# A planned attention stage: keeping VectorE's and GpSimd's SBUF work apart, one scan for the states, new ranks

## The chip, the cores and the metric

One core of one Trainium2 chip. The metric is the device time of one execution in microseconds (us). The kernel before takes 622.71 us, the median of three runs (622.52 to 623.51).

## The reference, cut to what matters

A decaying linear attention is followed by two feed-forward layers, all in 32-bit floats. Batch 2, 8 heads, 768 steps, head size 64; after it 1536 tokens of width 512.

```python
for t in range(S):                       # attention, decay gamma per head
    state = gamma * state + outer(k[t], v[t])
    y[t] = scale * (q[t] @ state)
x = y as (1536, 512)
h = x @ w_in                             # 512 -> 2048
x = where(h > 0, h, exp(min(h, 0)) - 1) @ w_out        # 2048 -> 512
out = ((x @ w_a) * (x @ w_b)) @ w_o      # 512 -> 1536 -> 512
```

## The kernel before

The recurrence is cut into 6 chunks of 128 steps. Heads go in 8 pairs (4 pairs per batch), two heads on the 128 partitions. For a pair, `decay` (ScalarE, L405) scales the keys, `states` (TensorE, L412) makes the sum of each of the first five chunks in PSUM as a block of 64 columns, `first` (ScalarE, L422) copies the first block to SBUF, and `scan` (VectorE, L427) carries the decay over the other four with four instructions in a row. For each half of a pair (three chunks), `scores` (TensorE, L454) makes the products of queries and keys, `masked` (VectorE, L460) multiplies them by a decay mask, `result` (TensorE, L475 with the states and L481 with the values) sums the output in PSUM, and `decayed` (VectorE, L491) writes it to SBUF as `yf`. `part` then splits `yf` into a high part (ScalarE, L513) and a low part (GpSimd, L517, a subtraction that reads and writes SBUF); the two are the operand of the dense layers.

The dense layers multiply in three products per block (L579 to L581: high by high, high by low, low by high), each of 128 by 128 by 512. Their weights come as 64-bit words, and every tile of 128 by 512 has to be rebuilt in 32 bits: two ScalarE passes (L348, L349), then four VectorE passes whose operands all lie in SBUF, `clamp` (L353), `shift` (L357), `join` (L361), `total` (L368), then a ScalarE pass (L374, high part) and a GpSimd subtraction (L378, low part). A tile is fetched by `fetch` (SyncE's DMA queue, L343) into one of three buffers, which `join` sets free.

The order of the attention stage is computed by a planner (`Plan`, L79) while the program is built. Every step is an operation with an engine, a cost, a rank (its due time), what it follows and the buffers that it takes. `run` picks again and again the operation that can start first by its model; an operation of the same engine with a lower rank that could start within 0.25 us of it goes before it. The model only sets the order of instructions within each engine and in SyncE's queue `Q`; on the chip the engines wait for data and buffers alone. The planner holds the 8 pairs, the first 8 weight tiles (`2 * G`; four of `w1`, four of `w2`), and `tile_f`: the first four blocks of the first dense layer (48 products), ranks 100 and above, which fill in where TensorE has nothing else. A pair `p` has the base rank 6 + 5.6 p, weight tile j the rank `need(j)` (L335), its steps some way before that. The cost model knows nothing of one engine slowing another.

After the planner, the dense loops run (`moe`, L705) with their own order by hand. They rebuild the other 60 weight tiles (`w_steps`, L183) between the products, with the tiles fetched by `w_load` (L172), up to three ahead.

Of the kernel before, what the change touches and what calls it, by code (L numbers as in the profile page):

```python
# [19 lines left out]
P = 128  # L20
C = 128
# [51 lines left out]
class Op:  # L73
    def __init__(self, engine, cost, rank, emit, after, takes, users):
        self.engine, self.cost, self.rank, self.emit = engine, cost, rank, emit
        self.after, self.takes, self.users, self.end = after, takes, users, None


class Plan:  # L79
# [4 lines left out]


    LAG = {"Q": 1.6}

    def __init__(self):
        self.ops = []

    def op(self, engine, cost, rank, emit, after=(), takes=(), uses=()):

        o = Op(engine, cost, rank, emit, [a for a in after if a], [t[0] for t in takes], [t[1] for t in takes])
        for users in [*o.users, *uses]:
            users.append(o)
        self.ops.append(o)
        return o
# [14 lines left out]
    def run(self, begin):  # L112
        clock, left = dict(begin), list(self.ops)
        while left:
            best = None
            for o in left:
                t = self.ready(o)
                if t is None:
                    continue
                t = max(t, clock[o.engine])  # L120
                key = (t, o.rank)
                if best is None or key < best[0]:
                    best = key, o
            (t, _), o = best

            for p in left:
                if p.engine == o.engine and p.rank < o.rank:
                    tp = self.ready(p)
                    if tp is not None and max(tp, clock[o.engine]) <= t + 0.25:
                        o = p  # L130
            t = max(t, self.ready(o))
            picked = []
            for rings, users in zip(o.takes, o.users):
                ring = min((r for r in rings if r.free_at() is not None), key=lambda r: r.free_at())
                ring.homes.append(users)
                picked.append(ring)
            o.end = t + o.cost
            clock[o.engine] = o.end
            left.remove(o)
            o.emit(*picked)  # L140
        return clock
# [3 lines left out]
def tile_kernel(ctx: ExitStack, tc: tile.TileContext, qk, kv, w1, w2, wa, wb, wo, tab, out):  # L145
# [23 lines left out]
    state = {"loaded": 0, "split": 0, "read": 0, "freed": 0, "tick": 0, "quota": 0, "lag": 0, "room": NW // 2}  # L169
    NS = 3  # L170

# [84 lines left out]
    def attention():  # L256
        pool, PS = tc.tile_pool, bass.MemoryType.PSUM
        with (
# [9 lines left out]
            mask = cst.tile([P, H, C], F32, name="mask")  # L268
            zero = cst.tile([P, 3 * C], F32, name="zero")
            nc.vector.memset(zero, 0.0)  # L270
            causal = tb1[:, :C]
            rise = lambda h: tb1[:, C + h : C + h + 1]
# [5 lines left out]
            warm = ps_s.tile([P, 2, 512], F32, tag="sc", name="warm")  # L278
            for _ in range(2):
                nc.tensor.matmul(warm[:, 0, : 3 * C], zero[:, :C], zero, start=True, stop=True)  # L280

            plan = Plan()
            op = plan.op
            ring = {n: Ring(k) for n, k in dict(qk=3, kv=3, kd=2, a=3, st=2, yf=2, raw=3, da=2, dc=2, du=2, m=3, r=3).items()}
            rsc, ry, r0 = Ring(2), Ring(2), Ring(2)
# [48 lines left out]

            need = lambda j: 32.0 + 3.5 * j if j < G else 60.0 + 3.0 * (j - G)  # L335

            def weight(j):
# [41 lines left out]

                o = op("Q", 1.3, n - 14, fetch, takes=[([ring["raw"]], raw_)])  # L380
                o = op("ACT", 1.3, n - 8, words, [o], [([ring["da"]], a_), ([ring["dc"]], c_)], [raw_])
                o = op("DVE", 0.5, n - 7, clamp, [o], uses=[a_])
                o = op("DVE", 0.6, n - 6.5, shift, [o], uses=[a_])
                o = op("DVE", 0.9, n - 6, join, [o], [([ring["du"]], u_)], [a_, raw_])
                o = op("DVE", 0.8, n - 5, total, [o], uses=[u_, c_])
                o = op("ACT", 0.6, n - 4, high, [o], uses=[u_])
                done["w", key] = op("POOL", 1.3, n - 3, low, [o], uses=[u_])


            def pair(p):  # L390
                b, hp = divmod(p, NHP)
                z = base(p)
                if b == 0:
                    done["mask", hp] = op(
                        "ACT", 0.7, z - 4,
                        lambda: [nc.scalar.mul(mask[:, h], causal, rise(h)) for h in (2 * hp, 2 * hp + 1)], [t1_],
                    )
                Q, K = users["qk", p], users["kv", p]
                kd_, s_, st_ = [], [], []

                def decay():
                    kd = tile_of(("kd", p), at, [P, NCH, 2, D], "kd")
                    k_ = T["kv", p][:, 0].rearrange("p (c h d) -> p c h d", c=NCH, h=2)
                    for h in range(2):
                        nc.scalar.mul(kd[:, :, h, :], k_[:, :, h, :], gk(2 * hp + h))  # L405

                def states(r):
                    ps = (ps_y if r is ry else ps0).tile([P, 512], F32, tag="y" if r is ry else "p", name="yk")
                    T["s", p] = ps = ps[:, : (NCH - 1) * D].rearrange("p (c d) -> p c d", d=D)
                    for c in range(NCH - 1):  # L410
                        for h in range(2):
                            nc.tensor.matmul(  # L412
                                ps[h * D : (h + 1) * D, c, :],
                                T["kd", p][:, c, h, :],
                                T["kv", p][:, 1, c * P + h * D : c * P + (h + 1) * D],
                                start=True,
                                stop=True,
                            )

                def first(*_):  # L420
                    st = tile_of(("st", p), at, [P, NCH - 1, D], "st")
                    nc.scalar.copy(st[:, 0, :], T["s", p][:, 0, :])  # L422

                def scan():
                    st, ps = T["st", p], T["s", p]
                    for c in range(1, NCH - 1):
                        nc.vector.scalar_tensor_tensor(  # L427
                            out=st[:, c, :], in0=st[:, c - 1, :], scalar=gc(hp), in1=ps[:, c, :],
                            op0=ALU.mult, op1=ALU.add,
                        )  # L430

                o = op("ACT", 1.15, z - 3, lambda *_: decay(), [done["k", p], t1_], [([ring["kd"]], kd_)], [K])
                o = op("PE", 0.75, z + 1, states, [o, done["v", p]], [([ry, r0], s_)], [kd_, K])
                o = op("ACT", 0.3, z + 1.1, first, [o], [([ring["st"]], st_)], [s_])
                done["st", p] = op("DVE", 1.25, z + 1.5, scan, [o], uses=[st_, s_])

                for half in range(2):
                    half_of(p, half, st_)

            def half_of(p, half, st_):  # L440
# [26 lines left out]
                def result(r):  # L467
# [3 lines left out]
                    for i in range(3):  # L471
                        c = half * 3 + i
                        for h in range(2 if c else 0):
                            r_ = slice(h * D, (h + 1) * D)
                            nc.tensor.matmul(  # L475
                                y[r_, i, :], st[r_, c - 1, :], q_[r_, c * C : (c + 1) * C], start=(c in (1, 3)), stop=False
                            )
# [21 lines left out]
                o = op("DVE", 0.95, z + 0.5, masked, [o, done["mask", hp]], [([ring["a"]], a_)], [sc_])  # L499
                o = op("PE", 1.5 + 0.2 * half, z + 6.5, result, [o, done["st", p]], [([ry, r0], y_)], [a_, st_, Q, K])  # L500
                done["y", key] = o
# [7 lines left out]
            def part(p, blk, key, o, yf_, cols, from_, rank):  # L509
# [10 lines left out]
                o = op("ACT", 0.2 + n / 1280, rank, high, [o, blk == NB - 1 and done["y", (NHP - 1, 1)]], uses=[yf_])  # L520
                done["x", blk, key] = op("POOL", 0.25 + n / 500, rank, low, [o], uses=[yf_])


            def tile_f(f, rank):
# [38 lines left out]
                o = op("ACT", 0.6, 43 + rank, high, [o], uses=[r_])  # L563
                op("POOL", 1.3, 45 + rank, low, [o], uses=[r_])

            with pool(name="atA", bufs=3) as atA:
                for p in range(NPAIR):
                    pair(p)
                for j in range(2 * G):
                    weight(j)  # L570
                for f in range(G):
                    tile_f(f, 4 * f)
                plan.run({"Q": 2.2, "PE": 4.2, "DVE": 1.4, "ACT": 2.3, "POOL": 0.4})
            state.update(loaded=2 * G, split=2 * G, read=2 * G)

# [188 lines left out]
```

## Time and profile before

| | |
|---|---|
| median of three runs | 622.71 us |
| profiled execution, its own time | 623.38 us |
| its span, first to last instruction | 621.6 us |
| TensorE busy in the span | 610.1 us, 98% |
| VectorE, ScalarE, GpSimd busy | 359.8, 285.4, 255.7 us |
| mean granted TensorE clock | 0.994 |

The profile is that of one execution; 1.8 us of its time lie outside of the span. A matmul's record ends with the end of its pipeline, so that records overlap: the distance between starts is what it costs in a row of others. The rows of a timeline begin with the start and the duration in us; in brackets stands how long the engine was idle before, and what ended that. A 32-bit matmul of the attention leaves two records.

### The profile page before, as it was taken

What the parts mean: (1) busy time and instruction counts of PE and PEld (TensorE: products, weight loads), DVE (VectorE), ACT (ScalarE), POOL (GpSimd) and SP (SyncE); (2) the same over time, 40 slices, a digit from 0 to 9 for tenths busy, and PEclk for the clock granted to TensorE, in tenths of its full rate; (3) what the DMA queues carried; (4) which work ended last, traced back from release to release, by engine and by line L of the source; (5) the groups of instructions that cost most, each with busy time, mean ns of one, the idle gap of its engine ahead of it and who ended that gap; (6) DMA issues with size and microseconds to landing.
All of it is one profiled execution on the core that took longest, in us unless ns stands there. A gap on an engine that the chain in (4) does not pass through costs nothing.

```text
span 621.6 us, 8081 instructions
## 1 busy us (share of the span) xinstructions
PE 610.1 (98%) x3168; PEld 503.5 (81%) x3168; DVE 359.8 (58%) x482; ACT 285.4 (46%) x514; POOL 255.7 (41%) x192
## 2 busy tenths in 40 slices
PE   7989899999999999999999999999999999999997
PEld 5867688888888888888888888888888888888886
DVE  2899856787784378528891282767065677211122
ACT  4574776778554457536752253444242444121110
POOL 0355654566455236516774352435133334311110
PEclk9999899999999999999999999999999999999999
DMA  8972413333321033202330031233022130001002
GB/s 325 408 280 67 130 39 97 103 102 102 102 74 62 1 102 101 69 1 69 101 101 2 1 100 37 71 98 101 1 67 69 49 93 30 0 2 51 18 34 102
DMA packets 14838, 52.24 MB, mean 84 GB/s; under 512 B 1616, under 2 KB 2512, under 8 KB 14800
## 3 DMA queue, kind: packets, MB, share of 16 engines
q1 hardware_dynamic: 14368, 50.99, 25.6%
q10 hardware_dynamic: 432, 0.73, 0.3%
q8 instruction: 25, 0.41, 0.3%
q14 instruction: 13, 0.11, 0.1%
HBM read 48.57 MB, written 3.15 MB: 83 GB/s over the span
## 4 chain that ended last, share of the span: by engine, by line
PE 91%; DVE 5%; DMA 1%; issue 1%; ACT 0%; SPq 0%; DVEq 0%
PE p L579 30%; PE p L581 30%; PE p L580 30%; DMA qk<-in_qk 1%; PE sc L454 1%; DVE a L460 1%; DVE yf L491 1%; DVE a L357 1%; DVE st L427 1%; DVE a L353 1%; PE yk L481 1%; DVE u L368 1%; PE yk L475 1%; DVE u L361 1%; SPq L315 0%
## 5 line engine op out<-in xcount | busy, mean ns | idle before, releaser
L603 POOL TENSOR_TENSOR gl<-pr,gh 128x512 fp32r<-128x512 f32 x36 | 50.5, 1403 | 156.9 <-ACT gh L601 156.9
L579 PE MATMUL p<-yh,wh 128*128 128x512 f32 x288 | 112.0, 389 | 0.0
L580 PE MATMUL p<-yl,wh 128*128 128x512 f32 x288 | 112.0, 389 | 0.0
L581 PE MATMUL p<-yh,wl 128*128 128x512 f32 x288 | 112.0, 389 | 0.0
L208 POOL TENSOR_TENSOR wl<-u,wh 128x512 fp32r<-128x512 f32 x60 | 88.3, 1472 | 51.7 <-ACT wh L206 50.8
L603 POOL TENSOR_TENSOR gl<-r,gh 128x512 fp32r<-128x512 f32 x44 | 67.2, 1528 | 81.4 <-ACT gh L601 81.4
L667 DVE TENSOR_TENSOR pr<-p,sa 128x512 f32<-128x512 f32 x36 | 24.9, 691 | 111.2 <-PE p L581 111.2
L201 DVE CUSTOM_DVE_ANT_0 u<-u,c 128x1024 uint16<-128x1024 uint16 x60 | 77.3, 1288 | 2.8
L579 PE MATMUL p<-xh,wh 128*128 128x512 f32 x192 | 75.6, 394 | 2.0 <-DVE r L546 2.0
L581 PE MATMUL p<-xh,wl 128*128 128x512 f32 x192 | 75.4, 393 | 0.0
L580 PE MATMUL p<-xl,wh 128*128 128x512 f32 x192 | 75.2, 392 | 0.0
L579 PE MATMUL p<-gh,wh 128*128 128x512 f32 x192 | 74.7, 389 | 0.0
L580 PE MATMUL p<-gl,wh 128*128 128x512 f32 x192 | 74.7, 389 | 0.0
L581 PE MATMUL p<-gh,wl 128*128 128x512 f32 x192 | 74.7, 389 | 0.0
L194 DVE TENSOR_SCALAR a<-a 128x512 f32<-128x512 f32 x60 | 65.3, 1088 | 15.9 <-ACT a L190 15.7
L601 ACT CAST gh<-pr 128x512 fp32r<-128x512 f32 x36 | 22.4, 621 | 101.5 <-DVE pr L667 101.5
L580 PEld LDWEIGHTS p<-yl,wh 128*128 128x128 f32 x288 | 54.1, 188 | 11.3
L579 PEld LDWEIGHTS p<-yh,wh 128*128 128x128 f32 x288 | 54.1, 188 | 11.2
L581 PEld LDWEIGHTS p<-yh,wl 128*128 128x128 f32 x288 | 54.1, 188 | 11.1
L580 PE MATMUL p<-wl,gh 128*128 128x512 f32 (+1 forms) x148 | 56.7, 383 | 0.0
L581 PE MATMUL p<-wh,gl 128*128 128x512 f32 (+1 forms) x148 | 56.7, 383 | 0.0
L579 PE MATMUL p<-wh,gh 128*128 128x512 f32 (+1 forms) x148 | 56.7, 383 | 0.0
(63 smaller groups left out, 946.6 us busy)
## 6 DMA issues: line engine op xcount, KB each, us to landing
raw<-in_w SPq DMA_DIRECT2D x32, 512.0 KB, 3.6
raw<-in_wa SPq DMA_DIRECT2D x12, 512.0 KB, 3.8
raw<-in_wb SPq DMA_DIRECT2D x12, 512.0 KB, 3.7
raw<-in_wo SPq DMA_DIRECT2D x12, 512.0 KB, 3.8
qk<-in_qk SPq DMA_DIRECT2D x7, 768.0 KB, 6.6
kv<-in_kv SPq DMA_DIRECT2D x7, 768.0 KB, 9.1
out<-oacc SPq DMA_DIRECT2D x11, 256.0 KB, 2.0
qk<-in_qk SPq DMA_DIRECT2D x2, 384.0 KB, 5.1
```

Of the source, the lines that this page charges most:

```text
L194: nc.vector.tensor_scalar(a, a, E_LO, E_HI, op0=ALU.max, op1=ALU.min)
L201: nc.vector.tensor_tensor(out=u, in0=u, in1=c, op=ALU.add)
L208: nc.gpsimd.tensor_tensor(out=lo, in0=t, in1=hi.bitcast(F32), op=ALU.subtract)
L353: nc.vector.tensor_scalar(a, a, E_LO, E_HI, op0=ALU.max, op1=ALU.min)
L357: nc.vector.tensor_single_scalar(ai, ai, 3, op=ALU.logical_shift_left)
L361: nc.vector.scalar_tensor_tensor(out=u, in0=T["raw", j][:, :, 1], scalar=SIGN, in1=T["da", j].bitcast(I32), op0=ALU.bitwise_and, op1=ALU.b ...
L579: nc.tensor.matmul(ps, lh, rh, start=first, stop=False)
L580: nc.tensor.matmul(ps, lh, rl, start=False, stop=False)
L581: nc.tensor.matmul(ps, ll, rh, start=False, stop=last)
L601: nc.scalar.copy(hi, t)
L603: nc.gpsimd.tensor_tensor(out=lo, in0=t, in1=hi.bitcast(F32), op=ALU.subtract)
L667: nc.vector.tensor_tensor(out=pr, in0=pb, in1=sa, op=ALU.mult)
```

## The change

- The planner knows a port: VectorE's four weight passes and all of GpSimd's subtractions are marked with it, and no two marked operations may overlap in its clock. On the chip no wait is added; what changes is the order in each engine.
- A TensorE operation of a rank below 100 may not be taken while it is more than 3 ranks above the lowest rank left on TensorE. An operation of a lower rank goes first if it could start within 0.1 us (before 0.25).
- The states of a pair come from one scan instruction of VectorE over 320 elements, which reads PSUM and a row of rates. For that `states` writes them with the chunk as the innermost index (a step of 20 bytes), the states lie so in SBUF too, and `result` reads them with that step as its stationary operand. ScalarE's copy of the first block goes; a ScalarE operation that writes the rates of a pair (`rate`, 320 elements) comes.
- `need` becomes 22 + 4.5 j for the first four weight tiles (before 32 + 3.5 j) and is lowered by 10 for the next four. 11 tiles are fetched in the planner (before 8); 8 are still rebuilt there.
- The costs in the model are lowered a little for the weight passes, and the six warm-up products of 128 columns stand for two of 384.

```diff
+    AHEAD, FILL = 3, 100
...
     def run(self, begin):
-        clock, left = dict(begin), list(self.ops)
+        clock, left = dict(begin, port=0.0), list(self.ops)
+        open_ = lambda o: max(clock[o.engine], clock["port"] + 0.05 if o.port else 0.0)
         while left:
             best = None
+            last = min((o.rank for o in left if o.engine == "PE"), default=0) + self.AHEAD
+            far = lambda o: o.engine == "PE" and last < o.rank < self.FILL
             for o in left:
                 t = self.ready(o)
-                if t is None:
+                if t is None or far(o):
                     continue
-                t = max(t, clock[o.engine])
+                t = max(t, open_(o))
...
-                if p.engine == o.engine and p.rank < o.rank:
+                if p.engine == o.engine and p.rank < o.rank and not far(p):
                     tp = self.ready(p)
-                    if tp is not None and max(tp, clock[o.engine]) <= t + 0.25:
+                    if tp is not None and max(tp, open_(p)) <= t + 0.1:
                         o = p
-            t = max(t, self.ready(o))
+            t = max(t, self.ready(o), open_(o))
...
             clock[o.engine] = o.end
+            if o.port:
+                clock["port"] = o.end
...
-    NS = 3
+    NS, NPL = 3, 8
...
-            zero = cst.tile([P, 3 * C], F32, name="zero")
+            zero = cst.tile([P, C], F32, name="zero")
             nc.vector.memset(zero, 0.0)
+
+            one = cst.tile([P, D * (NCH - 1)], F32, name="one")
+            nc.vector.memset(one, 1.0)
+            nc.vector.memset(one.rearrange("p (d c) -> p d c", c=NCH - 1)[:, :, 0], 0.0)
...
-            for _ in range(2):
-                nc.tensor.matmul(warm[:, 0, : 3 * C], zero[:, :C], zero, start=True, stop=True)
+            for i in range(6):
+                nc.tensor.matmul(warm[:, 0, i % 3 * C : (i % 3 + 1) * C], zero, zero, start=True, stop=True)
...
-            need = lambda j: 32.0 + 3.5 * j if j < G else 60.0 + 3.0 * (j - G)
+            need = lambda j: 22.0 + 4.5 * j if j < G else 50.0 + 3.0 * (j - G)
...
                 o = op("Q", 1.3, n - 14, fetch, takes=[([ring["raw"]], raw_)])
+                if j >= NPL:
+                    raw[key] = j
+                    return
                 o = op("ACT", 1.3, n - 8, words, [o], [([ring["da"]], a_), ([ring["dc"]], c_)], [raw_])
-                o = op("DVE", 0.5, n - 7, clamp, [o], uses=[a_])
-                o = op("DVE", 0.6, n - 6.5, shift, [o], uses=[a_])
-                o = op("DVE", 0.9, n - 6, join, [o], [([ring["du"]], u_)], [a_, raw_])
-                o = op("DVE", 0.8, n - 5, total, [o], uses=[u_, c_])
+                o = op("DVE", 0.44, n - 7, clamp, [o], uses=[a_], port=True)
+                o = op("DVE", 0.44, n - 6.5, shift, [o], uses=[a_], port=True)
+                o = op("DVE", 0.7, n - 6, join, [o], [([ring["du"]], u_)], [a_, raw_], True)
+                o = op("DVE", 0.65, n - 5, total, [o], uses=[u_, c_], port=True)
                 o = op("ACT", 0.6, n - 4, high, [o], uses=[u_])
-                done["w", key] = op("POOL", 1.3, n - 3, low, [o], uses=[u_])
+                done["w", key] = op("POOL", 1.3, n - 3, low, [o], uses=[u_], port=True)
...
-                    T["s", p] = ps = ps[:, : (NCH - 1) * D].rearrange("p (c d) -> p c d", d=D)
+                    T["s", p] = ps = ps[:, : (NCH - 1) * D]
+                    ps = ps.rearrange("p (d c) -> p d c", c=NCH - 1)
...
-                                ps[h * D : (h + 1) * D, c, :],
+                                ps[h * D : (h + 1) * D, :, c],
...
+                def rate(*_):
+                    nc.scalar.mul(tile_of(("keep", p), at, [P, D * (NCH - 1)], "keep"), one, gc(hp))
+
+                def scan(*_):
+
+                    st = tile_of(("st", p), at, [P, D, NCH - 1], "st")
+                    nc.vector.tensor_tensor_scan(
+                        st.rearrange("p d c -> p (d c)"), T["keep", p], T["s", p], 0.0, ALU.mult, ALU.add
+                    )
...
+                e = op("ACT", 0.55, z - 2.5, rate, [t1_], [([ring["keep"]], ke_)])
                 o = op("PE", 0.75, z + 1, states, [o, done["v", p]], [([ry, r0], s_)], [kd_, K])
-                o = op("ACT", 0.3, z + 1.1, first, [o], [([ring["st"]], st_)], [s_])
-                done["st", p] = op("DVE", 1.25, z + 1.5, scan, [o], uses=[st_, s_])
+                done["st", p] = op("DVE", 0.81, z + 1.5, scan, [o, e], [([ring["st"]], st_)], [s_, ke_])
...
-                                y[r_, i, :], st[r_, c - 1, :], q_[r_, c * C : (c + 1) * C], start=(c in (1, 3)), stop=False
+                                y[r_, i, :], st[r_, :, c - 1], q_[r_, c * C : (c + 1) * C], start=(c in (1, 3)), stop=False
...
-                for j in range(2 * G):
+                for j in range(NPL + NS):
                     weight(j)
...
-            state.update(loaded=2 * G, split=2 * G, read=2 * G)
+            raw.update({k: T["raw", j] for k, j in raw.items()})
+            state.update(loaded=NPL + NS, split=NPL, read=NPL)
```

## Rows read from the trace of the kernel before

**Rows 1.** Busy time by stretch: stretch, length, PE, PEld, DVE, ACT, POOL busy (instructions), clock, DMA share, GB/s.

```profile
16.00:24.00 8.00, 8.00 (x134) 6.71 (x132) 5.57 (x13) 4.10 (x11) 3.15 (x4) 1.00 1.01 409
24.00:66.86 42.86, 38.33 (x520) 30.95 (x517) 40.87 (x72) 25.52 (x57) 22.65 (x26) 0.96 0.57 207
...
38.60:47.60 9.00, 6.87 (x92) 5.71 (x94) 8.11 (x15) 6.10 (x14) 4.91 (x6) 0.81 0.52 183
...
100.00:200.00 100.00, 100.00 (x443) 82.81 (x442) 75.52 (x97) 67.00 (x116) 55.85 (x38) 1.00 0.31 90
```

**Rows 2.** TensorE's waits from 16 to 67 us: total us, times, longest.

```profile
PE p L579 <- DVE r L546: 2.0, 1, 2.0
PE sc L454 <- DVE a L460: 1.8, 2, 1.3
```

**Rows 3.** Timeline of TensorE around its idle time at 44 us.

```profile
36.04 0.80 PE L412 MATMUL yk<-kv,kd 128*64 128x64 f32 x20
36.77 0.65 PE L475 MATMUL yk<-qk,st 64*64 64x128 f32 x8
...
38.72 0.94 PE L454 MATMUL sc<-qk 64*128 64x128 f32 x12 [0.49 <-DVE a L460]
...
44.41 1.65 PE L454 MATMUL sc<-qk 64*128 64x128 f32 x12 [1.34 <-DVE a L460]
45.98 1.33 PE L412 MATMUL yk<-kv,kd 128*64 128x64 f32 x20
```

**Rows 4.** Timeline of TensorE after its idle time at 65 us, first dense products.

```profile
67.91 0.43 PE L580 MATMUL p<-xl,wh 128*128 128x512 f32 x1
...
71.55 0.40 PE L580 MATMUL p<-xl,wh 128*128 128x512 f32 x1
```

**Rows 5.** VectorE's groups from 0 to 76 us: busy us, mean ns of one, idle before.

```profile
L491 DVE TENSOR_TENSOR yf<-yk,gy 128x384 f32<-128x384 f32 x16 | 8.8, 550 | 2.4 <-PE yk L481 2.1
L361 DVE SCALAR_TENSOR_TENSOR u<-raw,a 128x512 int32<-128x512 int32 x8 | 8.1, 1006 | 0.8 <-issue 0.5
L368 DVE CUSTOM_DVE_ANT_0 u<-u,c 128x1024 uint16<-128x1024 uint16 x8 | 7.5, 939 | 0.2
L353 DVE TENSOR_SCALAR a<-a 128x512 f32<-128x512 f32 x8 | 6.2, 780 | 0.0
L357 DVE TENSOR_SCALAR a<-a 128x512 int32<-128x512 int32 x8 | 5.7, 716 | 0.1
```

**Rows 6.** Timeline of VectorE and GpSimd: passes beside each other, and passes alone.

```profile
27.52 0.41 DVE L357 TENSOR_SCALAR a<-a 128x512 int32<-128x512 int32 x1
27.96 0.69 DVE L361 SCALAR_TENSOR_TENSOR u<-raw,a 128x512 int32<-128x512 int32 x1
28.22 1.30 POOL L517 TENSOR_TENSOR xl<-yf,xh 128x384 fp32r<-128x384 f32 x1 [1.37 <-ACT xh L513]
28.57 1.22 DVE L427 SCALAR_TENSOR_TENSOR st<-st,tb,yk 128x64 f32<-128x64 f32 x4
...
38.53 1.28 POOL L378 TENSOR_TENSOR wl<-u,wh 128x512 fp32r<-128x512 f32 x1 [1.28 <-ACT wh L374]
38.59 1.50 DVE L353 TENSOR_SCALAR a<-a 128x512 f32<-128x512 f32 x1
...
42.79 0.69 DVE L368 CUSTOM_DVE_ANT_0 u<-u,c 128x1024 uint16<-128x1024 uint16 x1
```

**Rows 7.** ScalarE's groups from 0 to 67 us: busy us, mean ns of one, idle before.

```profile
L405 ACT ACTIVATE kd<-kv,tb 128x384 f32<-128x384 f32 x16 | 8.9, 607 | 4.0 <-DMA kv<-in_kv 4.0
L348 ACT ACTIVATE a<-raw 128x512 f32<-128x512 f32 x7 | 4.7, 674 | 0.0
L374 ACT CAST wh<-u 128x512 fp32r<-128x512 f32 x6 | 3.7, 620 | 4.7 <-DVE u L368 4.6
```

**Rows 8.** Timeline: pair 4's keys after their transfer, and its states.

```profile
26.39 1.12 ACT L405 ACTIVATE kd<-kv,tb 128x384 f32<-128x384 f32 x2 [0.47 <-DMA kv<-in_kv]
...
32.01 0.75 PE L412 MATMUL yk<-kv,kd 128*64 128x64 f32 x20
```

More of the change, by code (lines that the diff above doesn't have):

```diff
@@ L73, with __init__ @@
 class Op:
-    def __init__(self, engine, cost, rank, emit, after, takes, users):
+    def __init__(self, engine, cost, rank, emit, after, takes, users, port):
         self.engine, self.cost, self.rank, self.emit = engine, cost, rank, emit
-        self.after, self.takes, self.users, self.end = after, takes, users, None
+        self.after, self.takes, self.users, self.port, self.end = after, takes, users, port, None
 class Plan:
+    AHEAD, FILL = 3, 100
     LAG = {"Q": 1.6}
@@ L89, in __init__, with op @@
         self.ops = []
-    def op(self, engine, cost, rank, emit, after=(), takes=(), uses=()):
-        o = Op(engine, cost, rank, emit, [a for a in after if a], [t[0] for t in takes], [t[1] for t in takes])
+    def op(self, engine, cost, rank, emit, after=(), takes=(), uses=(), port=False):
+        o = Op(engine, cost, rank, emit, [a for a in after if a], [t[0] for t in takes], [t[1] for t in takes], port)
         for users in [*o.users, *uses]:
@@ L278, in attention @@
             warm = ps_s.tile([P, 2, 512], F32, tag="sc", name="warm")
-            for _ in range(2):
-                nc.tensor.matmul(warm[:, 0, : 3 * C], zero[:, :C], zero, start=True, stop=True)
+            for i in range(6):
+                nc.tensor.matmul(warm[:, 0, i % 3 * C : (i % 3 + 1) * C], zero, zero, start=True, stop=True)
             plan = Plan()
             op = plan.op
-            ring = {n: Ring(k) for n, k in dict(qk=3, kv=3, kd=2, a=3, st=2, yf=2, raw=3, da=2, dc=2, du=2, m=3, r=3).items()}
+            ring = {n: Ring(k) for n, k in dict(qk=3, kv=3, kd=2, keep=2, a=3, st=2, yf=2, raw=3, da=2, dc=2, du=2, m=3, r=3).items()}
             rsc, ry, r0 = Ring(2), Ring(2), Ring(2)
@@ L398, in pair @@
                 Q, K = users["qk", p], users["kv", p]
-                kd_, s_, st_ = [], [], []
+                kd_, s_, st_, ke_ = [], [], [], []
                 def decay():
@@ L418, in states @@
                             )
[L420 to L430, printed above, removed]
+                def rate(*_):
[5 more added lines that the diff above has]
+                    )
                 o = op("ACT", 1.15, z - 3, lambda *_: decay(), [done["k", p], t1_], [([ring["kd"]], kd_)], [K])
+                e = op("ACT", 0.55, z - 2.5, rate, [t1_], [([ring["keep"]], ke_)])
                 o = op("PE", 0.75, z + 1, states, [o, done["v", p]], [([ry, r0], s_)], [kd_, K])
-                o = op("ACT", 0.3, z + 1.1, first, [o], [([ring["st"]], st_)], [s_])
-                done["st", p] = op("DVE", 1.25, z + 1.5, scan, [o], uses=[st_, s_])
+                done["st", p] = op("DVE", 0.81, z + 1.5, scan, [o, e], [([ring["st"]], st_)], [s_, ke_])
                 for half in range(2):
@@ L499, in half_of @@
                 o = op("DVE", 0.95, z + 0.5, masked, [o, done["mask", hp]], [([ring["a"]], a_)], [sc_])
-                o = op("PE", 1.5 + 0.2 * half, z + 6.5, result, [o, done["st", p]], [([ry, r0], y_)], [a_, st_, Q, K])
+                o = op("PE", 1.45 + 0.25 * half, z + 6.5, result, [o, done["st", p]], [([ry, r0], y_)], [a_, st_, Q, K])
                 done["y", key] = o
@@ L520, in part @@
                 o = op("ACT", 0.2 + n / 1280, rank, high, [o, blk == NB - 1 and done["y", (NHP - 1, 1)]], uses=[yf_])
-                done["x", blk, key] = op("POOL", 0.25 + n / 500, rank, low, [o], uses=[yf_])
+                done["x", blk, key] = op("POOL", 0.25 + n / 500, rank, low, [o], uses=[yf_], port=True)
             def tile_f(f, rank):
@@ L563, in tile_f @@
                 o = op("ACT", 0.6, 43 + rank, high, [o], uses=[r_])
-                op("POOL", 1.3, 45 + rank, low, [o], uses=[r_])
+                op("POOL", 1.3, 45 + rank, low, [o], uses=[r_], port=True)
             with pool(name="atA", bufs=3) as atA:
```

## The prediction

> **What bounds the kernel now.** I read the busy time by stretch first, over all of the span. From 100 to 200 us TensorE is busy for all 100.00 us and passes 443 products, 0.2257 us each [rows 1]; the other engines have gaps there. So the dense loops run at the pace of their products. The diff touches none of these products, and it leaves their weights at least as early (eight tiles rebuilt, three more fetched). That part can only shift as a block, and whatever the change is worth lies ahead of it, where TensorE stands still or runs slowly.
>
> The same view shows where that is. From 24 to 66.86 us TensorE is busy for 38.33 of 42.86 us, so it stands for 4.53 us, while VectorE is busy for 40.87 us, 95% [rows 1]. TensorE's waits name VectorE as the end of 2.0 us (the first dense blocks, whose PSUM waits for `larger`) and of 1.8 us (the scores, whose PSUM waits for `masked`) [rows 2]. VectorE is the engine that ends last in this stage, and TensorE is second, with little to spare.
>
> The waits have a second price. [...] The timeline has the sizes: 12 score records take 1.65 us at 44.41 against 0.94 at 38.72, and 20 records of `states` 1.33 against 0.80 at 36.04 [rows 3]. That is 0.71 + 0.53 = 1.24 us lost after idle times of 0.49 and 1.34 us. After the wait of 2.0 us it comes again, in the first dense products: from 67.91 to 71.55 us the trace has nine starts to starts, 3.64 us where nine of 0.2257 are 2.03 [rows 4], 1.61 us lost.
>
> So what VectorE's lateness costs TensorE is 4.53 + 1.24 + 1.61 = 7.4 us. This is the most that the middle and the end of the stage can give back.
>
> **The change part by part.** *Keeping the port apart.* Groups by line: the four weight passes, eight of each up to 76 us, took 8.1 + 7.5 + 6.2 + 5.7 = 27.5 us on VectorE [rows 5]. Alone they take 0.69 (L361), 0.69 (L368) and 0.41 (L357) [rows 6]; L353, of the same size and with one input too, I price like L357. Eight tiles alone are 8 x 2.20 = 17.6 us, so 9.9 us of VectorE's time are excess. The timeline shows what it is: L353 started 0.06 us after a GpSimd pass and took 1.50 us, ending 0.28 us after GpSimd's end, as if it had begun only then. The four state instructions (L427), which read PSUM, took their 1.22 us beside a GpSimd pass of 1.30 us [rows 6]. So it is the passes on SBUF alone that are held up, and while VectorE is held up its PSUM work stands in line behind, in order. An order that puts PSUM work beside GpSimd's passes saves up to 9.9 us, and nothing if the engines drift from the model's clock, since no wait enforces it. I take two thirds, 6.6 us: the model's new costs (0.44, 0.44, 0.70, 0.65) are close to the durations alone, and waits for data pull the engines together at every half pair.
>
> *One scan.* Four instructions of L427 take 1.22 us [rows 6]. The one that replaces them reads 320 elements from PSUM and 320 from SBUF. From below it is bounded by L491, which also reads a PSUM and an SBUF operand and takes 0.55 us for 384 [rows 5]; from above by the 1.22 us of the chain that it replaces. It is one instruction like the first and hands a value on like the second, so I take the middle, 0.88: 0.34 us saved for a pair, 2.7 us for eight (0 to 5.4). [...] ScalarE loses a copy on the way from the products to the scan and gains `rate`, at most the 0.61 us of a scaled 384-element pass [rows 7], 4.9 us for eight. It has 42.86 - 25.52 = 17 us idle from 24 to 66.86 us [rows 1], and `rate` waits for nothing but its constants and its buffer, so I put it at nothing; in a wrong place it holds up `decay`, by 0.61 us a time.
>
> *New ranks.* Weights 0 to 3 come 7 to 10 ranks earlier, 4 to 7 ten ranks earlier; ranks run about as us do (5.6 for a pair). VectorE was idle for 8.00 - 5.57 = 2.4 us from 16 to 24 us [rows 1], which the first tile can use now. SyncE's queue is sorted by the same ranks, so up to two more weight fetches pass the loads of pairs 3 and 4. At 409 GB/s [rows 1] one of 512 KB takes 1.28 us. Pair 4's keys were at ScalarE at 26.39 us just as they landed and were done at 27.51; `states` took them at 32.01 [rows 8]. That cover of 4.5 us is more than 2.6, so the fetches cost nothing; without it TensorE would wait for the rest. The three further fetches fall in the end of the stage, where the transfers are at half load (0.52 from 38.6 to 47.6 us) [rows 1].
>
> *The sum on VectorE.* 6.6 + 2.7 + 2.4 = 11.7 us of relief, against TensorE's loss of 7.4 us. VectorE then stops being the engine that ends last, TensorE is, and its waits and slow stretches go. I keep 1.0 us for two waits of the size of the 0.49 us one [rows 3]: the limit of 3 ranks takes away a filling that was used (the `states` of pair 7, rank 46.2, ran at 45.98 ahead of a result of rank 40.5), so that a wait for VectorE has less to cover it.
>
> *The stride.* `states` writes PSUM and `result` reads its stationary operand with a step of 20 bytes. No row of TensorE shows such a step. The nearest is ScalarE's pass over one word of two (674 ns) beside one over 512 contiguous words (620 ns) [rows 7], 9% more. The products on the states take 0.65 us for 8 records [rows 3], 1.63 for the 20 of a pair, the writing 0.75 to 0.80. 9% on both is 0.2 us a pair, 1.7 us; on the reading alone 1.2. Nothing makes it a gain: there are as many records and columns. From above, a doubling is 19 us. I take 1.0 us, since part of a load lies beside the product before it (the 12 loads and 12 products of a row overlap).
>
> *The start.* The smaller `zero`, the second memset and the six warm-up products have as many columns as before, ahead of the first load's arrival: nothing. The slow clock at the beginning may end one stretch earlier or later; I give that the 1.24 us of the first slow stretch on each side.
>
> **Sum.** 7.4 - 1.0 - 1.0 = 5.4 us. The profiled execution took 623.38 us, its span 621.6; like it the changed kernel would take 618.0 us with a span of 616.2. That execution lies 0.67 us above the median of the runs, so the median goes from 622.7 to 617.3 us.
>
> **The rivals.** *The engines drift.* Little of the 9.9 us goes, since on the chip nothing keeps the passes apart and the first late transfer moves one engine against the other. Then relief is 2.7 + 2.4 = 5.1 us, TensorE still waits near 40 or at the end, and one slow stretch stays: 5.1 - 1.0 - 1.0 - 1.2 = 1.9 us gained, 620.8. For it: no wait is added. Against it: VectorE was never late before 24 us in the old order, and the relief is spread over all tiles.
>
> *A transfer comes too late.* The fetches that pass a pair use up its cover, TensorE waits for one fetch (1.28 us) and runs slowly after it (1.24 us): 617.3 + 2.5 = 619.8. Against it the 4.5 us above.
>
> *The stride decides: slower.* Every column of a stepped operand costs more; if the products on the states alone double, that is 8 x 1.63 = 13 us of TensorE's time in a stage that TensorE bounds by then: 622.7 - 7.4 + 1.0 + 13 = 629. It decides from 6.4 us on, 0.8 us a pair, a third of the 2.4 that reading and writing take. Such a price is in no row; 9% is what the nearest shows. [...]
>
> **How the numbers follow.** The forecast has 0.54, with a range of its own from 614 (no wait and no price of the stride left, 622.7 - 7.4, and the start 1.2 better) to 619.3. Drift has 0.19, the late transfer 0.09, the stride 0.13, and 0.05 goes to a change that moves nothing. Faster by over 0.2% (1.2 us, about what a measurement of this kernel can tell) gets the forecast, most of drift and of the late transfer: 0.78. The same gets 0.08, slower 0.14, the stride and a bit of drift with TensorE held back by the 3 ranks. The range is 614 to 622: it leaves out the stride's case and a little below.
>
> **What would show it.** After: L353 to L368 near 2.2 us a tile instead of 3.4; one scan of 0.6 to 1.0 us; no wait of TensorE on `masked` or `larger` over 0.5 us and the first dense products all 0.23 us apart; the dense loop beginning earlier and unchanged in pace. Wrong, if the 20 records of `states` or the products on the states take clearly longer at full clock, if TensorE's waits name a transfer or ScalarE's `rate`, or if the weight passes are as long as before.

## The result, and the profile after

The changed kernel takes 615.4 us, the median of four runs (614.91 to 616.99), beside 622.62 us of the kernel before. The ratio is 0.9893, with a 95% interval from 0.9862 to 0.9924: about 6.7 us faster (the medians differ by 7.2). A second set of five runs gave 616.09 us and 0.9891 [0.9872, 0.9909]. The forecast was 617.3, with a range from 614 to 622. The profiled execution took 615.63 us, its span is 613.8, where before it was 621.6.

First the busy time by stretch, the same as in [rows 1]: stretch, length, PE, PEld, DVE, ACT, POOL busy (instructions), clock, DMA share, GB/s.

```profile
16.00:24.00 8.00, 8.00 (x138) 7.16 (x137) 6.96 (x12) 3.96 (x9) 3.05 (x4) 1.00 1.02 413
...
24.00:66.86 42.86, 42.86 (x543) 35.87 (x540) 38.20 (x58) 30.47 (x64) 26.77 (x28) 1.00 0.60 224
...
100.00:200.00 100.00, 100.00 (x443) 82.83 (x442) 70.37 (x91) 61.46 (x108) 51.39 (x35) 1.00 0.30 85
```

TensorE stands for nothing from 24 to 66.86 us, where it stood for 4.53 us, and the granted clock is 1.00, where it was 0.96. VectorE is busier from 16 to 24 us (6.96 against 5.57) and less busy after that (38.20 against 40.87). The dense loop is as before, 443 products in 100 us.

TensorE's waits after 11 us are one line, and it lies ahead of the stretches of [rows 2]:

```profile
PE yk L493 <- DVE st L446: 1.0, 1, 1.0
```

VectorE's groups from 0 to 76 us, as in [rows 5] (busy us, mean ns of one, idle before):

```profile
L509 DVE TENSOR_TENSOR yf<-yk,gy 128x384 f32<-128x384 f32 x16 | 8.7, 547 | 4.7 <-PE yk L499 4.0 <-POOL xl L535 0.4 <-issue 0.2
L377 DVE SCALAR_TENSOR_TENSOR u<-raw,a 128x512 int32<-128x512 int32 x8 | 7.1, 888 | 0.3
L446 DVE TENSOR_TENSOR_SCAN st<-keep,yk 128x320 f32<-128x320 f32 x8 | 6.5, 810 | 1.0 <-PE yk L432 1.0
L384 DVE CUSTOM_DVE_ANT_0 u<-u,c 128x1024 uint16<-128x1024 uint16 x8 | 6.0, 750 | 0.5
L373 DVE TENSOR_SCALAR a<-a 128x512 int32<-128x512 int32 x8 | 5.5, 684 | 0.2
L369 DVE TENSOR_SCALAR a<-a 128x512 f32<-128x512 f32 x8 | 4.0, 504 | 0.0
```

The four passes are L369, L373, L377 and L384 now. They sum to 22.6 us, where they were 27.5, and 17.6 alone. A scan takes 0.81 us. VectorE now waits more for TensorE: `yf` stands 4.0 us for its products, where it was 2.1. Of the 4.0 us, 1.3 lie after 16 us, where it was 0.5.

And TensorE's timeline where [rows 3] had the idle time and the slow clock:

```profile
36.10 0.80 PE L432 MATMUL yk<-kv,kd 128*64 128x64 f32 x20
36.83 0.72 PE L493 MATMUL yk<-qk,st 64*64 64x128 f32 x8
37.48 0.88 PE L499 MATMUL yk<-a,kv 128*64 128x128 f32 x12
...
43.91 0.94 PE L472 MATMUL sc<-qk 64*128 64x128 f32 x12
44.77 0.95 PE L493 MATMUL yk<-qk,st 64*64 64x128 f32 x12
45.65 0.88 PE L499 MATMUL yk<-a,kv 128*64 128x128 f32 x12
```

No idle time, and 12 score records take 0.94 us near 44 us as well, where they took 1.65. The products on the states (L493) have got dearer: 8 records from start to start 36.83 to 37.48, 0.65 us.

### The profile page after: what moved, and what is told of

Its sections match the earlier page's. It is cut to its first block, busy times and chain, and to the rows that moved or that the text cites. A ratio compares the mean times of both kernels' runs of the same rounds, so it can differ in the third digit from the quotient of the medians.

```text
span 613.8 us, 8076 instructions
## 1 busy us (share of the span) xinstructions
PE 606.8 (99%) x3176; PEld 504.3 (82%) x3176; DVE 352.7 (57%) x460; ACT 287.3 (47%) x514; POOL 256.6 (42%) x192
## 4 chain that ended last, share of the span: by engine, by line
PE 98%; DMA 1%; DVE 0%; SPq 0%; issue 0%; DVEq 0%
PE p L598 30%; PE p L599 30%; PE p L600 30%; PE sc L472 2%; PE yk L499 2%; PE yk L493 2%; DMA qk<-in_qk 1%; PE yk L432 1%; DVE st L446 0%; SPq L331 0%; DVE oacc L712 0%; DVEq L446 0%
## 5 line engine op out<-in xcount | busy, mean ns | idle before, releaser
L206 DVE TENSOR_SCALAR a<-a 128x512 f32<-128x512 f32 x60 | 64.1, 1069 | 14.6 <-ACT a L202 14.4
```

Of the source, the lines that this page charges most:

```text
L206: nc.vector.tensor_scalar(a, a, E_LO, E_HI, op0=ALU.max, op1=ALU.min)
```

## The experiments

Two theories stood against each other at the start. Mine: VectorE's passes on SBUF are held up beside GpSimd's subtractions, VectorE is late for that, and TensorE waits; an order that keeps them apart removes it. The rival: the other parts do it (the ranks, the limit, the scan), or the order by itself, and the hold-ups are by the way. A ratio compares with the kernel before as it ran beside the experiment; its median there was 621.66 to 623.29 us, so that ratios, and not times, go together across the groups. "The passes" are VectorE's four weight passes, summed over the eight tiles of the stage.

### The change without one of its parts

Without the port in the planner's model:

```diff
-        self.after, self.takes, self.users, self.port, self.end = after, takes, users, port, None
+        self.after, self.takes, self.users, self.port, self.end = after, takes, users, False, None
```

> The changed kernel with the port taken out of the planner's model (no operation is marked; all else as changed). My theory: the order that keeps VectorE's SBUF passes and GpSimd's apart is the largest part of VectorE's relief (the four passes sum to 22.6 us in the changed kernel, 27.5 before), so without it the passes take 26 to 28 us again, VectorE is late for TensorE at least once, and the kernel takes 617.5 to 620 us. Rival (the ranks do it: weights that are rebuilt earlier meet idle time, the port is by the way): under 616.5 us, no wait of TensorE on VectorE over 0.5 us.

Measured: 621.66 us (10 runs), ratio to the kernel before 0.9994 [0.9974, 1.0015]. All of the gain is gone, more than I expected, though the passes sum to 24.0 us, less than I expected. What matters is where they are held up. TensorE's waits from 16 to 67 us, and the stretch that ends with the longest, VectorE and GpSimd in the order of time:

```profile
PE p L598 <- DVE r L564: 3.1, 1, 3.1
PE yk L493 <- DVE st L446: 0.7, 1, 0.7
PE sc L472 <- DVE a L478: 0.4, 1, 0.4
```

```profile
61.80 1.60 DVE L377 SCALAR_TENSOR_TENSOR u<-raw,a 128x512 int32<-128x512 int32 x1
63.54 0.99 DVE L384 CUSTOM_DVE_ANT_0 u<-u,c 128x1024 uint16<-128x1024 uint16 x1
64.45 0.54 DVE L509 TENSOR_TENSOR yf<-yk,gy 128x384 f32<-128x384 f32 x1
64.92 0.67 DVE L564 SCALAR_TENSOR_TENSOR r<-m,p 128x512 f32<-128x512 f32 x1
...
61.31 1.54 POOL L394 TENSOR_TENSOR wl<-u,wh 128x512 fp32r<-128x512 f32 x1 [1.28 <-ACT wh L390]
62.81 2.03 POOL L535 TENSOR_TENSOR xl<-yf,xh 128x256 fp32r<-128x256 f32 x2
```

`larger` (L564), which sets PSUM free for the next dense block, stands behind two passes that are held up: 1.60 us for 0.69, and 0.99 for 0.69. TensorE waits 3.1 us for it. These two hold-ups are 1.2 of the 3.1 us; where the rest comes from, this run doesn't show by itself (`n_fill` below has the same order without GpSimd's subtractions).

With the old ranks of the weights:

```diff
-            need = lambda j: 22.0 + 4.5 * j if j < G else 50.0 + 3.0 * (j - G)
+            need = lambda j: 32.0 + 3.5 * j if j < G else 60.0 + 3.0 * (j - G)
```

> The changed kernel with the old ranks of the weights (32 + 3.5 j, 60 + 3 (j - 4)). My theory: 1 to 2 us are lost since weight tiles pile up at the end of the stage, 616.5 to 617.5 us, TensorE waiting there only. Rival (the ranks do it): 619 to 621 us, TensorE's waits near 40 us and at the end as in the kernel before.

Measured: 617.55 us (5 runs), 0.9937 [0.9916, 0.9958], about 2 to 3 us behind the changed kernel; TensorE waits for `masked` 0.7 us and for a state 0.3 near 43 us, where I expected no wait, and for `larger` 0.4 at the end. The middle between the two theories, nearer to mine: the ranks are worth some 2 to 3 us on top of the port.

Without the limit of 3 ranks:

```diff
-    AHEAD, FILL = 3, 100
+    AHEAD, FILL = 1000, 100
```

> The changed kernel without the limit of 3 ranks on TensorE's order. My theory: within 0.7 us of the changed kernel (614.7 to 616.1), since with VectorE in time the order by rank is TensorE's order anyhow. Rival (the limit is what keeps TensorE's waits away, because work taken ahead fills PSUM and lets VectorE's work pile up): 617 us or more, waits of TensorE of 1 us and over.

Measured: 615.47 us (4 runs), 0.9906 [0.9885, 0.9928]. No difference from the changed kernel is seen, and the four passes sum to 22.6 us here too: this part is not needed.

With the four instructions for the states, contiguous states and ScalarE's copy:

```diff
...
-                    nc.vector.tensor_tensor_scan(
-                        st.rearrange("p d c -> p (d c)"), T["keep", p], T["s", p], 0.0, ALU.mult, ALU.add
-                    )
+                    for c in range(1, NCH - 1):
+                        nc.vector.scalar_tensor_tensor(
+                            out=st[:, c, :], in0=st[:, c - 1, :], scalar=gc(hp), in1=ps[:, c, :],
+                            op0=ALU.mult, op1=ALU.add,
+                        )
...
```

> The changed kernel with the four instructions for the states and ScalarE's copy of the first, states contiguous for TensorE again. My theory: TensorE's products on the states come back from 0.65 and 0.88 us start to start to 0.58 and 0.80 (1.2 us over all pairs gained), VectorE gets 8 x 0.41 = 3.3 us more work; as it had some 3 us to spare, the sum is between 614 and 616.5 us. Rival (the scan is a main source of the gain): 618 us or more, TensorE waiting for masked or for the states.

Measured: 617.49 us (6 runs), 0.9940 [0.9919, 0.9961]. One us above my range: TensorE waits for `masked` 2.2 us, near 32 and 39 us, and for `larger` 0.5, so VectorE had less to spare than I took it to have.

### One part alone

The port in the kernel before (marks, the model's clock, the lower costs of the passes):

```diff
-                t = max(t, clock[o.engine])
+                t = max(t, open_(o))
...
-                op("POOL", 1.3, 45 + rank, low, [o], uses=[r_])
+                op("POOL", 1.3, 45 + rank, low, [o], uses=[r_], port=True)
```

> The kernel before with the port in the planner's model alone (marks, the model's clock, the passes' lower costs). My theory: VectorE's passes fall from 27.5 to 22 to 24 us and TensorE gets back 2 to 4 us of its 7.4: 618.5 to 620.5 us. Rival (the engines drift, the model's port does nothing): 621.5 to 623 us, passes at 26 us or more.

Measured: 619.97 us (10 runs), 0.9967 [0.9950, 0.9984]. The time is as expected, the passes are not: 29 of the 32 take 23.9 us up to 76 us, where alone they would take 15.8, and the last three come after that. The hold-ups moved and hardly got fewer; TensorE waits 3.6 us for `masked`, 3.1 of it at once.

The ranks alone:

```diff
-            need = lambda j: 32.0 + 3.5 * j if j < G else 60.0 + 3.0 * (j - G)
+            need = lambda j: 22.0 + 4.5 * j if j < G else 50.0 + 3.0 * (j - G)
```

> The kernel before with the new ranks of the weights alone. My theory: the 2.4 us that VectorE idles up to 24 us are used, 619.5 to 621.5 us, passes still at 26 us or more. Rival (the ranks do it): 616 to 618 us.

Measured: 622.21 us (10 runs), 0.9999 [0.9989, 1.0010], passes 26.2 us. The time is above my range, and nothing is gained: the weights meet idle time early (VectorE is busy for 23.41 us of the 24 from 16 to 40 us, where it was 20.90), and TensorE waits elsewhere (2.3 us on `masked`, 1.8 on `larger`, 1.6 on a `yf`).

The scan alone (with the smaller `zero`, which makes room for the rates):

```diff
-                    for c in range(1, NCH - 1):
-                        nc.vector.scalar_tensor_tensor(
...
+                    nc.vector.tensor_tensor_scan(
+                        st.rearrange("p d c -> p (d c)"), T["keep", p], T["s", p], 0.0, ALU.mult, ALU.add
+                    )
...
```

> The kernel before with the one scan, its rates and stepped states alone (and the smaller zero tile, which makes room). My theory: VectorE gets 3.3 us back, TensorE loses 1.2 us to the step, so 620.5 to 622 us. Rival (the scan is a main source): under 619 us.

Measured: 620.46 us (10 runs), 0.9976 [0.9965, 0.9987], at the lower edge of what I expected; the passes take 26.5 us.

So the parts don't add up. Alone they give about 2.0 us (port), 1.5 (scan) and nothing (ranks). The port with one of the others gives about 4, all three give 6.7, the scan and the ranks without the port nothing. (The runs from the changed kernel's side also hold its small parts: the 0.1 us for a lower rank, the three further fetches, the limit.)

### The hold-up by itself

The kernel before, in its own order, with GpSimd's subtractions of the planned stage replaced by fills that read nothing (the other two places likewise):

```diff
-                    nc.gpsimd.tensor_tensor(out=lo, in0=T["du", j].bitcast(F32), in1=hi.bitcast(F32), op=ALU.subtract)
+                    nc.gpsimd.memset(lo.bitcast(F32), 0.0)
```

> The kernel before, its order untouched, with GpSimd's subtractions of the planned stage (L378, L517, L557) replaced by fills with zero, which read nothing; so the low parts of these operands are left out of the result. My theory (it is VectorE's passes being held up beside GpSimd's subtractions that makes TensorE wait): the four passes fall from 27.5 to under 20 us, TensorE's waits after 16 us fall from 4.5 to under 2 us, 615.5 to 618.5 us without any change of order. Rival (the order itself is what the port in the model improves, the hold-ups are by the way): 620.5 us or more.

Measured: 615.59 us (4 runs), 0.9887 [0.9858, 0.9917]. The old order, planned with no knowledge of a port, is as fast as the changed kernel once GpSimd's subtractions are gone. Its groups on VectorE, and TensorE's waits from 16 to 67 us:

```profile
L361 DVE SCALAR_TENSOR_TENSOR u<-raw,a 128x512 int32<-128x512 int32 x8 | 5.5, 691 | 0.2
L368 DVE CUSTOM_DVE_ANT_0 u<-u,c 128x1024 uint16<-128x1024 uint16 x8 | 5.5, 686 | 0.2
L357 DVE TENSOR_SCALAR a<-a 128x512 int32<-128x512 int32 x8 | 3.8, 474 | 0.1
L353 DVE TENSOR_SCALAR a<-a 128x512 f32<-128x512 f32 x8 | 3.4, 420 | 0.0
```

```profile
PE sc L454 <- DVE a L460: 1.3, 2, 0.9
PE yk L412 <- ACT kd L405: 0.2, 1, 0.2
```

The passes are at 18.2 us against 27.5 in [rows 5], and the waits at 1.5 us, where 4.53 us stood idle. The fills are shorter than subtractions (0.31 to 0.59 us) and wait for no data, so GpSimd is early too; but from 16 to 67 us no listed wait of TensorE, ScalarE or VectorE in the kernel before names GpSimd.

The order of the change without the port, with the same fills:

> The changed kernel without the port in the model, its order untouched, with the same fills in place of GpSimd's subtractions of the planned stage (the low parts are left out of the result). My theory: without hold-ups that order is as good as the changed kernel's, 613.5 to 616.5 us, passes under 20 us. Rival (that order is a bad one in itself): 619 us or more.

Measured: 615.78 us (4 runs), 0.9883 [0.9860, 0.9906]. TensorE has no wait after 16 us, the passes sum to 17.7 us. The order that gave 621.66 us is not a bad one in itself: without the subtractions nothing of its wait of 3.1 us on `larger` is left.

The other way round, the changed kernel's order with GpSimd's weight subtraction done twice:

```diff
                     nc.gpsimd.tensor_tensor(out=lo, in0=T["du", j].bitcast(F32), in1=hi.bitcast(F32), op=ALU.subtract)
+                    nc.gpsimd.tensor_tensor(out=lo, in0=T["du", j].bitcast(F32), in1=hi.bitcast(F32), op=ALU.subtract)
```

> The changed kernel, its order untouched, with GpSimd's subtraction for each of the eight weight tiles done twice in a row, of which the planner knows nothing. My theory: the passes meet GpSimd's again, 25 us or more in all, and TensorE waits for VectorE again: 617 to 621 us. Rival (a plan with one scan and the new ranks has room enough, whatever GpSimd does): 615 to 616.5 us, no wait of TensorE over 0.5 us after 16 us.

Measured: 618.1 us (4 runs), 0.9923 [0.9896, 0.9949], passes 26.1 us. The interval overlaps both of the changed kernel's, so the loss of 2 us is not settled by the time alone; its four runs (617.84 to 618.58) lie above the four of `n_fill` beside them (615.15 to 616.33). TensorE's waits from 16 to 67 us, where the changed kernel has none:

```profile
PE sc L473 <- DVE a L479: 2.0, 2, 1.4
PE yk L494 <- DVE st L447: 0.2, 1, 0.2
```

Both directions agree: without GpSimd's subtractions both orders lose their waits or most of them, and with more subtractions TensorE waits for VectorE again. But their sum is not the measure: this kernel keeps 4.8 us of the gain at 26.1 us of passes, and `a_noport` has none of it at 24.0. So the port in the model is a way to an order whose hold-ups, of which half are left (22.6 us against 17.6 alone), stand where TensorE does not need what is behind them.

### What bounds it now

TensorE bounds the changed kernel from 11 us on, so the start is left. Idle stretches of it were filled with products of zeros into unused columns:

```diff
...
+                    if p == 0:
+                        for _ in range(4 if half == 0 else 2):
+                            nc.tensor.matmul(sc[:, 0, 3 * C :], zero, zero, start=True, stop=True)
```

> The changed kernel with idle stretches of TensorE in the first 11 us filled by products of zeros into unused columns of the scores' PSUM: 8 instead of 6 warm-up products, and 4, 2 and 4 more after the scores and the states of pair 0. My theory: TensorE, which now bounds all of the span, runs at half clock until about 16.5 us; if the fill lets the clock rise near 8 us and keeps it, 1 to 3 us come back, 612.5 to 614.5 us. Rival (the start is bound by transfers and by the fill's own time): 615 to 616.5 us.

> The changed kernel once more, beside the one above on the same chip: 614.9 to 617 us by both theories, ratio to the kernel before 0.987 to 0.992.

Measured: 615.0 us (5 runs), 0.9873 [0.9854, 0.9893], beside 616.09 us and 0.9891 [0.9872, 0.9909] for the changed kernel on the same chip. The intervals overlap, so no gain is shown, and the time lies in the rival's range and not in mine; the spans of the two profiled executions are 613.3 and 613.7 us. Yet the slow start is gone. TensorE's start, and ScalarE's wait for the keys from 14 to 40 us:

```profile
4.81 0.94 PE L475 MATMUL sc<-qk 64*128 64x128 f32 x12
5.68 1.16 PE L480 MATMUL sc<-zero 128*128 128x128 f32 x8
...
14.26 0.95 PE L499 MATMUL yk<-qk,st 64*64 64x128 f32 x12
```

```profile
ACT kd L424 <- DMA kv<-in_kv: 7.9, 5, 3.3
```

The first scores take 0.94 us (in the changed kernel 1.65), and the products that began at 16.68 us there begin at 14.26. That this is the clock is read from the durations: the profile's granted clock is 1.00 up to 16 us in both kernels, but 1.65 us is what the 12 scores took at 44.41 us in the kernel before, where the granted clock from 44.40 to 47.20 us is 0.50. Then ScalarE waits for transfers for 7.9 us, where it waited 0.3, and the lead of 2.4 us shrinks to 0.6 by the first dense product (51.33 against 51.92). TensorE loses it at the `states` of three pairs, which need the keys: from start to start they take 1.23, 1.12 and 1.23 us, where 0.68 to 0.73 is usual. The DMA share is 1.03 from 12 to 16 us already, so the transfers stand right behind TensorE.

## Why the prediction was right

The forecast was 617.3 us and the kernel takes 615.4. The mechanism held in the main, and the time that it gives back was put too low.

*What bounds it.* Right: TensorE stood for VectorE, and with VectorE in time the idle stretch, both waits and both slow stretches are gone. No wait after 16 us is left. Of the idle time, 0.49 and 0.18 us near 42 us name ScalarE's keys and not VectorE, which the prediction passed over. They go back to VectorE all the same, for ScalarE had itself waited for a `yf` just before:

```profile
40.59 0.60 ACT L513 CAST xh<-yf 128x128 fp32r<-128x128 f32 x2 [1.00 <-DVE yf L491]
41.10 2.13 ACT L405 ACTIVATE kd<-kv,tb 128x384 f32<-128x384 f32 x4
```

*The size of the loss: 7.4 us was too little.* I took idle times as the trace gives them, and they count from the end of a record, which lies after the start of the next in a full row. From start to start the gaps cost more. In the kernel before:

```profile
25.99 0.88 PE L481 MATMUL yk<-a,kv 128*64 128x128 f32 x12
26.70 0.75 PE L412 MATMUL yk<-kv,kd 128*64 128x64 f32 x20
27.38 0.94 PE L454 MATMUL sc<-qk 64*128 64x128 f32 x12
...
34.36 0.88 PE L481 MATMUL yk<-a,kv 128*64 128x128 f32 x12
35.17 0.94 PE L454 MATMUL sc<-qk 64*128 64x128 f32 x12
...
37.35 0.88 PE L481 MATMUL yk<-a,kv 128*64 128x128 f32 x12
...
40.39 0.88 PE L481 MATMUL yk<-a,kv 128*64 128x128 f32 x12
41.76 0.33 PE L412 MATMUL yk<-kv,kd 128*64 128x64 f32 x2 [0.49 <-ACT kd L405]
...
48.01 0.88 PE L481 MATMUL yk<-a,kv 128*64 128x128 f32 x12
...
64.51 0.39 PE L581 MATMUL p<-xh,wl 128*128 128x512 f32 x1
66.86 0.50 PE L579 MATMUL p<-xh,wh 128*128 128x512 f32 x1 [1.96 <-DVE r L546]
```

From 37.35 to 38.72 are 1.37 us, where 0.81 is usual before scores; from 40.39 to 41.76 are 1.37, where 0.71 is usual before `states`; from 41.76 to 44.41 are 2.65 for 0.68; and from 64.51 to 66.86 are 2.35 for 0.23. That is 5.3 us instead of 4.53. The slow stretches cost 1.42 us (44.41 to 48.01; the granted clock is 0.50 from 44.40 to 47.20) and 1.76 (66.86 to 71.55; granted 0.64) from start to start, 8.5 us in all.

*The stride: 1.0 us, measured 1.1 to 1.2.* The products on the states take 0.65 us for 8 records, 0.88 for 12 (39.16 to 40.04), from start to start; before it was 0.58 and 0.80. That is 0.15 us a pair, all on reading. The writing with a step shows no price for these blocks of 64 columns: 20 records from 36.10 to 36.83, 0.73 us as at 36.04 in [rows 3]. The 0.8 us a pair from which the stride would have decided shows in no run. In `b_scan` too the stepped kernel was the faster one (0.9976).

*The waits that I kept: 1.0 us, measured none.* With 0.2 us from an earlier start (the third pair's products on the states begin at 25.18 us, before at 25.41) the sum is 8.5 - 1.1 + 0.2 = 7.6; TensorE's last product begins 7.75 us earlier (610.34 against 618.09). The sum of the forecast was 5.4: it was short by the 1.1 us of the loss and the 1.0 us of waits that did not come.

*VectorE's sum: right in its outcome, wrong as a measure.* The passes lost 4.9 us (I took 6.6), a scan saved 0.41 (0.34), and the idle time from 16 to 24 us shrank by 1.4 (2.4): 9.6 us of 11.7. But the experiments show that relief doesn't convert into time by its sum. The passes of the kernel without the port are at 24.0 us: with its scan and its idle time from 16 to 40 us (22.91 us busy, where it was 20.90) that is 3.5 + 3.3 + 2.0 = 8.8 us of relief, more than the 7.4 us that I took for the loss, and it gains nothing. With the old scan the passes are at 23.7 and it gains 3.7. So that step of the prediction, relief larger than loss and therefore no waits, came out in part by luck; what decided is where the hold-ups fall, which it did not price. As far as the waits show, a hold-up costs where `masked`, a state or `larger` stands behind it on VectorE while TensorE has nothing else.

*The drift rival* was wrong: although no wait was added, six of eight tiles took 14.4 us up to 56 us, 2.4 each. After that the engines do meet (L373 takes 1.46 us, L377 1.36 in the last two), where no wait of TensorE follows. *The transfers* were in time, as the cover had it; the filled start shows that the margin is small, some 2 us. *The limit of 3 ranks*, for which I kept 1.0 us, shows neither a cost nor a gain. *`rate`* takes 0.55 us and stood 1.6 us for its buffer, but no wait of TensorE names it, so putting it at nothing was right.

*Left open:* why the scan's 1.5 us are gone in the run without the port, which has the ranks and the small parts too (0.9994 [0.9974, 1.0015], for the scan alone 0.9976 [0.9965, 0.9987]; the intervals overlap). Each order puts its hold-ups elsewhere, which the waits show; that this is chance was not tested. The 0.1 us in place of 0.25, the lower costs in the model and the three further fetches had no run of their own. And a fill is also shorter than a subtraction and sets buffers free earlier, so the fills show what GpSimd's subtractions cost in all, not the hold-ups of single passes.

## What to carry to other kernels

When two engines hold each other up, sum their excess to see whether there is something, but value it by what is queued behind each hold-up. Before writing a schedule around such a hold-up, measure what its absence is worth, by a stand-in on the other engine that reads nothing: here that run gave the whole gain (0.9887 against 0.9893), with the reservation that the stand-in is shorter as well. And take the cost of a wait from start to start of the records (here 5.3 us), not from the idle time (4.53), and add the slow clock after it (3.2).

## What the runs showed of the hardware

VectorE's passes with two SBUF inputs were not held up by GpSimd's fills in `b_fill`: L361 and L368 took 691 and 686 ns in the mean, and 1006 and 939 ns in the kernel before with its subtractions [rows 5]. Of the passes with one input, one L357 took 0.83 us beside fills, twice its 0.41 us alone [rows 6]. Among GpSimd's subtractions, one of 384 columns took 1.30 us beside L361 [rows 6], and 1.00 at 36.26 us of the changed kernel, where none of the four passes stood beside it. The rows are those of `b_fill`:

```profile
36.25 1.28 POOL L378 MEMSET wl<- 128x512 f32 x2
36.98 0.83 DVE L357 TENSOR_SCALAR a<-a 128x512 int32<-128x512 int32 x1
37.47 1.26 POOL L557 MEMSET gl<- 128x512 f32 x2
37.84 0.69 DVE L361 SCALAR_TENSOR_TENSOR u<-raw,a 128x512 int32<-128x512 int32 x1
38.67 0.69 DVE L368 CUSTOM_DVE_ANT_0 u<-u,c 128x1024 uint16<-128x1024 uint16 x1
38.68 0.52 POOL L378 MEMSET wl<- 128x512 f32 x1
```
